# Folding the output weights on array quarters, and another order of loads at the start, in a two-branch linear attention kernel

## The chip, the cores and the metric

The kernel runs on one core of one Trainium2 chip. The metric is the device time of one execution in microseconds. The kernel before takes 189.27 us (median of three executions, 189.26 to 189.87). All six of its executions, 188.97 to 189.87 us, agree within 0.5%. A difference counts as faster or slower when it is 2% or more, which is 3.8 us here.

## The reference

Two branches, A and B, read the same x (2048 tokens of 640 features). Each has its own weights and 32 heads of 20 features, and a gate mixes the results. Cut to what matters:

```python
def branch(x, wqkv, wo):                       # A and B alike
    q, k, v = split(x @ wqkv)                  # 32 heads, Dh = 20
    phi = lambda t: where(t > 0, t + 1, exp(t)) + 1e-6
    kv  = einsum("bhsd,bhse->bhde", phi(k), v) # 20 x 20 for each head
    z   = phi(k).sum over tokens
    o   = (phi(q) @ kv) / (phi(q) . z + 1e-6)
    return o @ wo
out = g * branch_A(x) + (1 - g) * branch_B(x)  # g = sigmoid(x . gate_w)
```

The tokens are divided into 16 tiles of 128. The kernel never makes o. For each branch it forms a 640 x 640 matrix W', the block-diagonal kv times wo, and then makes each output tile as scaled phi(q) times W'.

## The kernel before

A list of operations is handed to a small scheduler that orders them on each engine and assigns PSUM banks. Four parts matter here.

The left factor of W' (KVL) comes from five-step matmuls in units of 120 rows (six heads). VectorE masks it to block-diagonal form:

```python
for us in ((0, 1, 2, 3), (4, 5)):
    ...
    for i, u in enumerate(us):
        lo = GR * u if u < 5 else D - GR          # GR = 120
        for c in range(NC):                       # NC = 5
            e.matmul(PS[0:GR, ps.slot, GR*i : GR*i + GR], WV[X][:, c, lo:lo+GR],
                     gv[:, c, :, lo // 5 : lo // 5 + 24], ...)
    ...   # DVE tensor_tensor: KVL[X][:, us, :] = PSUM * mask
```

W' is one unit of 120 rows at a time. ScalarE copies a unit to WST, and one DMA (a "move") brings it into the layout of WP, in which five rows of WST become one row of 5 x 640:

```python
def wp_unit(X, u):
    e.matmul(a[0:GR, 0:512], KVL[X][:, u, :], WO[X][:, u, 0:512], start=True, stop=True)
    e.matmul(a[0:GR, 512:D], KVL[X][:, u, :], WO[X][:, u, 512:D], start=True, stop=True)
    ...   # ACT: WST[X][:, u, :] = PSUM
    dma("SP", ..., WP[X][lo//5 : hi//5, :, :], WST[X][r:GR, u, :], 1280 * (hi - lo), ...)
```

So a move writes 24 rows of WP and reads 120 rows of WST: 153.6 KB (the profile prints 150.0, in units of 1024 bytes). The last move is a third of that.

The order of branch B's end: the output tiles whose A half is made early ("parts", `o_part`) fill the time until WPB is complete.

```python
kv_unit("B"); o_part(4)
for u in range(NU):                # NU = 6
    wp_unit("B", u)
    if u % 2 == 0: o_part(5 + u // 2)
for t in range(8, NOA): o_part(t)  # NOA = 13; the first matmul on WPB comes right after
```

The start: x tiles 0 and 1 are transposed by TensorE, and the key weights of A arrive in five 128-row pieces.

```python
x_tp(0); warm(6, 1); k_step("A", 0, 0, pss[0])
x_tp(1); k_step("A", 0, 1, pss[0]); k_step("A", 1, 0, pss[1]); k_step("A", 1, 1, pss[1])
gate_col()                          # 5-row transpose of gate_w
... # the other steps of A tiles 0, 1; then B tiles 0, 1; then each tile for A and B
```

## Time and profile before

| | before |
|---|---|
| time | 189.27 us |
| profiled span | 187.4 us |
| TensorE busy | 184.8 us, 99% |
| first matmul on XN and PKA (end of the key stage) | 48.31 us |
| first matmul on WPB | 159.31 us |
| last matmul starts | 185.07 us |

"PE" is TensorE's matmuls and "PEld" its weight loads, which overlap them. The rows by slice cut the span into 40 parts; a digit is the busy share in tenths, and in PEclk the share of the full clock that was granted. A group line gives line, engine, operation, output<-inputs, shape, count, then busy us with mean ns of one, then the idle time just before these instructions and what ended it. A matmul's duration is longer than the distance to the next start (379 ns for 512 columns, with 215 to 216 ns between starts), so TensorE's work is counted by starts. Here are two slice rows and the two groups of output matmuls from the page of the kernel before, for later comparison:

```profile
PE   9999999999999999999999999999999999999995
...
PEclk9999999999999999999999999999999999999999
...
L903 PE MATMUL ps<-WPA,EX 128*128 128x512 bf16 x120 | 17.3, 299 | 0.0
L903 PE MATMUL ps<-WPB,PKA 128*128 128x512 bf16 x120 | 16.5, 299 | 0.0
```

TensorE has no slice below 90% until the end, the clock never falls, and the matmuls on WPB wait for nothing.

### The profile page before, as it was taken

How to read it: one execution, taken by the hardware profiler on the slowest of the kernel's cores; microseconds unless marked ns; L12 is line 12 of the kernel's file. 1: busy time of each engine (PE TensorE's matmuls, PEld its weight loads, DVE VectorE, ACT ScalarE, POOL GpSimd, SP SyncE). 2: the span in 40 equal slices, each digit the busy share in tenths (PEclk: the TensorE clock that was granted, in tenths of full speed). 3: DMA queues.
4: the chain of work that ended last, by engine and by line, in shares of the span. 5: the costliest groups of instructions: out<-in, count | busy, mean ns of one | idle time of the engine just before them, and what ended most of it. 6: DMA issues, size and time to landing. Idle time of an engine off the chain costs nothing.

```text
span 187.4 us, 3207 instructions
## 1 busy us (share of the span) xinstructions
PE 184.8 (99%) x1266; PEld 108.4 (58%) x1266; DVE 136.0 (73%) x263; ACT 94.5 (50%) x168; POOL 0.6 (0%) x7
## 2 busy tenths in 40 slices
PE   9999999999999999999999999999999999999995
PEld 5555555555566656655557556655566655555552
DVE  2489888878833546487798999879996999965600
ACT  3265655565554546644684667877624594100012
POOL 1000000000000000000000000000000000000000
PEclk9999999999999999999999999999999999999999
DMA  7989999999001011011501232540015365132322
GB/s 205 279 162 128 183 381 372 365 227 197 9 0 35 0 38 35 0 35 29 93 9 27 60 48 44 125 113 5 0 37 117 32 152 134 40 138 105 137 79 70
DMA packets 36301, 19.89 MB, mean 106 GB/s; under 512 B 25630, under 2 KB 36286, under 8 KB 36286
## 3 DMA queue, kind: packets, MB, share of 16 engines
q1 hardware_dynamic: 35844, 19.48, 42.9%
q8 instruction: 10, 0.16, 0.4%
q10 hardware_dynamic: 442, 0.20, 0.4%
q14 instruction: 5, 0.04, 0.1%
HBM read 9.39 MB, written 2.62 MB: 64 GB/s over the span
## 4 chain that ended last, share of the span: by engine, by line
PE 99%; DVE 0%; issue 0%; DVEq 0%
PE ps L903 23%; PE ps L743 23%; PE ps L508 19%; PE ps L617 18%; PE ps L618 5%; PE ps L509 5%; PE ps L659 2%; PE ps L442 1%; PE ps L697 1%; PE ps L455 1%; PE ps L698 0%; DVE TSB L947 0%; DVE ONE L372 0%; PE ps L489 0%; DVEq L230 0%
## 5 line engine op out<-in xcount | busy, mean ns | idle before, releaser
L508 PE MATMUL ps<-WKW,XT 128*128 128x512 bf16 x160 | 44.2, 381 | 0.0
L760 ACT ACTIVATE EK<-ps 128x512 bf16<-128x512 f32 x40 | 23.9, 598 | 31.6 <-PE ps L743 29.2
L509 PE MATMUL ps<-WKW,XT 128*128 128x128 bf16 (+1 forms) x160 | 35.2, 220 | 0.0
L541 ACT ACTIVATE EK<-ps 128x640 bf16<-128x640 f32 x32 | 22.3, 703 | 11.6 <-PE ps L509 5.7
L508 PEld LDWEIGHTS ps<-WKW,XT 128*128 128x128 bf16 x160 | 15.7, 98 | 18.9 <-DMA WKW<-in_A_wqkv_dram 0.4
L743 PE MATMUL ps<-XT,WQA 128*128 128x512 bf16 x100 | 24.5, 379 | 0.0
L743 PE MATMUL ps<-XT,WQB 128*128 128x512 bf16 x100 | 23.7, 379 | 0.0
L617 PE MATMUL ps<-XN,PKB 128*128 128x512 bf16 x80 | 23.5, 379 | 0.0
L617 PE MATMUL ps<-XN,PKA 128*128 128x512 bf16 x80 | 23.5, 379 | 0.0
L770 DVE TENSOR_SCALAR EK<-EK 128x512 bf16<-128x512 bf16 x40 | 11.6, 291 | 14.9 <-ACT EK L760 14.6
L618 PE MATMUL ps<-XN,PKA 128*128 128x129 bf16 x80 | 17.6, 220 | 0.0
L618 PE MATMUL ps<-XN,PKB 128*128 128x129 bf16 x80 | 17.6, 220 | 0.0
L903 PE MATMUL ps<-WPA,EX 128*128 128x512 bf16 x120 | 17.3, 299 | 0.0
L903 PE MATMUL ps<-WPB,PKA 128*128 128x512 bf16 x120 | 16.5, 299 | 0.0
L743 PEld LDWEIGHTS ps<-XT,WQB 128*128 128x128 bf16 x100 | 11.0, 118 | 8.5
L509 PEld LDWEIGHTS ps<-WKW,XT 128*128 128x128 bf16 x160 | 15.7, 98 | 0.0
L544 DVE TENSOR_SCALAR EK<-EK 128x640 bf16<-128x640 bf16 x32 | 10.4, 325 | 7.2 <-ACT EK L541 6.9
L743 PEld LDWEIGHTS ps<-XT,WQA 128*128 128x128 bf16 x100 | 10.7, 118 | 8.1
L617 PEld LDWEIGHTS ps<-XN,PKA 128*128 128x128 bf16 x80 | 9.4, 117 | 7.9
L617 PEld LDWEIGHTS ps<-XN,PKB 128*128 128x128 bf16 x80 | 9.4, 117 | 7.8
L949 ACT ACTIVATE TSB<-ps 128x640 bf16<-128x640 f32 (+1 forms) x3 | 2.0, 668 | 23.2 <-PE ps L903 23.2
L552 DVE SCALAR_TENSOR_TENSOR PKB<-ps,EK 128x640 bf16<-128x640 f32 x16 | 13.2, 825 | 0.6
(75 smaller groups left out, 240.6 us busy)
## 6 DMA issues: line engine op xcount, KB each, us to landing
out_dram<-TSB SPq DMA_DIRECT2D x15, 160.0 KB, 1.8
XN<-in_A_x_dram SPq DMA_DIRECT2D x1, 2240.0 KB, 8.8
WKW<-in_A_wqkv_dram SPq DMA_DIRECT2D x5, 160.0 KB, 4.1
WKW<-in_B_wqkv_dram SPq DMA_DIRECT2D x5, 160.0 KB, 4.3
WQA<-in_A_wqkv_dram SPq DMA_DIRECT2D x1, 800.0 KB, 10.5
WQB<-in_B_wqkv_dram SPq DMA_DIRECT2D x1, 800.0 KB, 13.2
WVA<-in_A_wqkv_dram SPq DMA_DIRECT2D x1, 800.0 KB, 12.7
WVB<-in_B_wqkv_dram SPq DMA_DIRECT2D x1, 800.0 KB, 14.2
```

What stands on the lines that cost most here:

```text
L508: e.matmul(a[:, 0:512], l, WK[X][:, c, 0:512], start=(c == 0), stop=(c == NC - 1))
L509: return e.matmul(a[:, 512:w], l, WK[X][:, c, 512:w], start=(c == 0), stop=(c == NC - 1))
L541: op("ACT", lambda e: e.activation(EK[:, ek.slot, :], psw(ps, D), ACT.Exp), act_cost(D), ins=[ps] + first, outs=[ek], name="ke")
L544: lambda e: e.tensor_scalar(EK[:, ek.slot, :], EK[:, ek.slot, :], 1.0, EPS, op0=ALU.min, op1=ALU.add),
L552: lambda e: e.scalar_tensor_tensor(PKt[X][:, t, :], psw(ps, D), 0.0, EK[:, ek.slot, :], op0=ALU.max, op1=ALU.add),
L617: e.matmul(a[:, 0:512], l, XN[:, t, 0:512], start=(t == 0), stop=(t == NT - 1))
L618: return e.matmul(a[:, 512 : D + 1], l, XN[:, t, 512 : D + 1], start=(t == 0), stop=(t == NT - 1))
L659: r = e.matmul(PS[0:GR, ps.slot, GR * i : GR * i + GR], WV[X][:, c, lo : lo + GR], gv[:, c, :, lo // 5 : lo // 5 + 24], start=(c == 0), st ...
L743: r = e.matmul(PS[:, ps.slot, :], WQ[X][:, c, g::5], XT[:, c, 512 * b : 512 * b + 512], start=(c == 0), stop=(c == NC - 1),)
L760: lambda e: e.activation(EQ[:, eq.slot, :], PS[:, ps.slot, :], ACT.Exp),
L770: lambda e: e.tensor_scalar(EQ[:, eq.slot, :], EQ[:, eq.slot, :], 1.0, EPS, op0=ALU.min, op1=ALU.add),
L903: r = e.matmul(a[:, l0 - lo : h0 - lo], PQ[X, b][:, g, 128 * (t % 4) : 128 * (t % 4) + 128], WP[X][:, g, l0:h0], start=(X == first and g = ...
```

## The change

The intent is to take work from TensorE, the bound. A W' unit uses 120 x 120 of the 128 x 128 array for a matrix that is zero outside 20 x 20 blocks. The change cuts W' into 11 tiles of 60 rows (the last 40), and works on four of them at once on the 64 x 64 quarters, in two bursts of 320 output columns per branch. The left factor gets padded rows so that a pair of tiles starts at partitions 0 and 64. The start is reordered, so that x tile 1 is loaded first on ScalarE's queue and transposed right behind tile 0. The gate column becomes a full-array matmul, and A's tile 2 comes before B's keys. In the diff, cuts are marked with `...`:

```diff
-    for u in range(NU):
-        wp_unit("B", u)
-        if u % 2 == 0:
-            o_part(5 + u // 2)
+    wp_burst("B", 0)
+    o_part(5)
+    o_part(6)
+    wp_burst("B", 1)
+    o_part(7)
...
-    NOA = 13
+    NOA = 14
...
+    def wp_burst(X, half):
+        ps = [Buf("wp", "ps", 2) for _ in range(2)]      # two pairs of banks
+        lo = HALF * half                                  # HALF = 320
+        def fn(e):
+            for k in range(3):
+                for a, b in ((0, 192), (192, HALF)) if k == 1 else ((0, HALF),):
+                    for t in range(4 * k, min(4 * k + 4, 11)):
+                        ...                               # c, r: which quarter
+                        x = e.matmul(o[:, HALF*k + a : HALF*k + b],
+                            KVL[X][64*r : 64*r + w, u, d : d + p],
+                            WO[X][64*r : 64*r + w, u, lo + a : lo + b], start=True, stop=True)
+        op("PE", fn, 640.0, ins=bkvl[X] + ...)            # all masks of the branch
+        ...                                               # ACT copies 124 x 960 to WST
+            if half == 0: continue
+            for t in ...:
+                h, m = 64 * (t // 2 % 2), 12 if t < 10 else 8
+                dma("ACT" if X == "B" and t in (1, 5, 9) else "SP", ...,
+                    WP[X][12*t : 12*t + m, :, :], WST[X][h : h + NC*m, 3*r + t//4, :], ...)
...
-                            PS[0:GR, ps.slot, GR * i : GR * i + GR],
-                            WV[X][:, c, lo : lo + GR],
+                            PS[0:n, ps.slot, GR * i : GR * i + NC * w],   # n = 128, last 104
+                            WV[X][:, c, lo : lo + n],
...
-    warm(6, 1)
-    k_step("A", 0, 0, pss[0])
+    warm(1, 1)
     x_tp(1)
-    k_step("A", 0, 1, pss[0])
-    k_step("A", 1, 0, pss[1])
-    k_step("A", 1, 1, pss[1])
+    for c in range(2):
+        for t in range(2):
+            k_step("A", t, c, pss[t])
...
-        op("PE", lambda e: e.transpose(tv(), GW5[:, :], IDN[0:NC, 0:NC]), ...)
+        op("PE", lambda e: e.matmul(tv(), GWZ[:, :], IDN[:, 0:NC], ...), ...)
```

Six moves of 24 rows become eleven of 12 rows (the last 8), all of them after the second burst, on two queues for branch B.

More of the change, by code (lines that the diff above doesn't have):

```diff
@@ L20 @@
 NU = 6
+HR = 60
+HALF = 320
 def _bf16_bits(a):
@@ L30, in _consts @@
     p = np.arange(128)[:, None]
-    bd = (p // 20 == np.arange(24)[None, :] // 4).astype(np.float32)
-    return _bf16_bits(bd)
-CW = 24
+    q, m = p % 64, np.arange(24)[None, :]
+    bd = np.where(p < 64, (q >= 4) & ((q - 4) // 20 == m // 4), (q < 60) & (3 + q // 20 == m // 4))
+    be = q // 20 == m[:, 0:8] // 4
+    return _bf16_bits(np.concatenate([bd, be], axis=1).astype(np.float32))
+CW = 32
 XS_W = 672
@@ L40, with __init__ @@
 class Buf:
-    def __init__(self, name, pool=None, n=1):
-        self.name, self.pool, self.n = name, pool, n
+    def __init__(self, name, pool=None, n=1, at=(0, 2, 4, 6)):
+        self.name, self.pool, self.n, self.at = name, pool, n, at
         self.writers, self.readers = [], []
@@ L107, in can @@
                 w = max(w, d.end + (HOP if d.eng != o.eng or d.dma else 0.0))
+            skip = set()
             for b in o.outs:
                 if b.pool and b.slot is None:
-                    got = self.pick(b, w)
+                    got = self.pick(b, w, skip)
                     if got is None:
@@ L113, in can @@
                     w = max(w, got[0])
+                    skip |= set(range(got[1], got[1] + b.n))
             return w
@@ L163, in run, with pick @@
         return max(o.end for o in self.ops)
-    def pick(self, b, t):
+    def pick(self, b, t, skip=()):
         pool = self.free[b.pool]
@@ L169, in pick @@
         for x in pool:
-            have[x[1]] = x[0]
+            if x[1] not in skip:
+                have[x[1]] = x[0]
         if b.n == 1:
-            if not pool:
+            if not have:
                 return None
@@ L176, in pick @@
             return best[0], best[3]
-        c = [(max(have[s], have[s + 1]), s) for s in have if s % 2 == 0 and s + 1 in have]
+        c = [(max(have[i] for i in range(s, s + b.n)), s) for s in b.at if all(i in have for i in range(s, s + b.n))]
         return min(c) if c else None
@@ L275, in body @@
     WQ = {X: sb("WQ" + X, [128, NC, D], bf) for X in XS}
-    WV = {X: sb("WV" + X, [128, NC, D], bf) for X in XS}
-    WO = {X: sb("WO" + X, [GR, NU, D], bf) for X in XS}
+    WV = {X: sb("WV" + X, [128, NC, D + 8], bf) for X in XS}
+    WO = {X: sb("WO" + X, [128, NU, D], bf) for X in XS}
     PK = {X: sb("PK" + X, [128, NT * D], bf) for X in XS}
@@ L296, in body @@
     GS = {X: sb("GS" + X, [128, NC, D], bf) for X in XS}
-    KVL = {X: sb("KVL" + X, [GR, NU, GR], bf) for X in XS}
-    WST = {X: WKW[0:GR, i * NU * D : (i + 1) * NU * D].rearrange("p (u f) -> p u f", u=NU) for i, X in enumerate(XS)}
+    KVL = {X: sb("KVL" + X, [128, NU, GR], bf) for X in XS}
+    WST = {X: WKW[:, i * NU * D : (i + 1) * NU * D].rearrange("p (u f) -> p u f", u=NU) for i, X in enumerate(XS)}
     WP = {X: sb("WP" + X, [128, NC, D], bf) for X in XS}
@@ L303, in body @@
     FXT = {"A": WV["A"][:, :, :].rearrange("p c f -> p (c f)")[:, 0:2048].rearrange("p (b s) -> p b s", b=NB), "B": XNf[:, 0:2048].rearrange("p (b s) -> p b s", b=NB)}
-    NOA = 13
+    NOA = 14
     OA = [XNf[:, 2048 + 1280 * i : 3328 + 1280 * i].bitcast(f32) for i in range(6)]
-    OA += [PK["B"][:, 1280 * i : 1280 * i + 1280].bitcast(f32) for i in range(7)]
+    OA += [PK["B"][:, 1280 * i : 1280 * i + 1280].bitcast(f32) for i in range(8)]
     NEK, NEQ, NOS = 4, 4, 4
@@ L318, in body @@
     CST = sb("CST", [128, CW], bf)
-    GW5 = sb("GW5", [NC, 128], bf)
+    GWZ = sb("GWZ", [128, 128], bf)
     GE = sb("GE", [128, NT], f32)
@@ L328, in body @@
     IDN = sb("IDN", [128, 128], bf)
-    BDM = CST[0:GR, 0:24]
+    BDM = CST[:, 0:24]
+    BDE = CST[64:104, 24:32]
     sch = Sched({"ps": 8, "ek": NEK, "eq": NEQ, "os": NOS})
@@ L369, in body @@
     bwv = {X: Buf("wv" + X) for X in XS}
-    bwo = {X: Buf("wo" + X) for X in XS}
+    bwo = {}
     op("DVE", lambda e: e.memset(ONE[:, :], 1.0), 120.0, outs=[bone], name="one")
@@ L385, in body @@
     )
+    bpad = {X: Buf("pad") for X in XS}
+    for X in XS:
+        op("POOL", lambda e, X=X: e.memset(WV[X][:, :, 0:4], 0.0), 100.0, outs=[bpad[X]], prio=10**6, name="wvpad")
+        op("POOL", lambda e, X=X: e.memset(WO[X][0:4, 0:5, :], 0.0), 1500.0, outs=[bpad[X]], prio=10**6, name="wopad")
+    zgw = op("POOL", lambda e: e.memset(GWZ[:, :], 0.0), 200.0, name="zgw")
     bxo = Buf("xo")
@@ L410, in body @@
     bgw = Buf("gw5")
+    ld_x("ACT", 1)
+    dma("ACT", "gw", GWZ[0:NC, :], gate_w.rearrange("(c p) -> c p", p=128), 1280, outs=[bgw], after=[zgw])
     dma("ACT", "cst", CST[:, :], cap[:, :], 128 * CW * 2, outs=[bcst])
-    ld_x("ACT", 1)
-    dma("ACT", "gw", GW5[:, :], gate_w.rearrange("(c p) -> c p", p=128), 1280, outs=[bgw])
     for c in range(NC):
@@ L417, in body @@
         ld_wk("SP", "A", c)
+    xt_dma(2, 3)
     for c in range(NC):
         ld_wk("SP", "B", c)
-    for t0, t1 in ((2, 3), (3, 4), (4, 5), (5, 6), (6, 8), (8, 12), (12, 16)):
+    for t0, t1 in ((3, 4), (4, 5), (5, 6), (6, 8), (8, 12), (12, 16)):
         xt_dma(t0, t1)
@@ L425, in body @@
     for X in XS:
-        dma("SP", "wv" + X, WV[X][:, :, :], w3(X, 2), 819200, outs=[bwv[X]])
+        dma("SP", "wv" + X, WV[X][:, :, 4 : D + 4], w3(X, 2), 819200, outs=[bwv[X]])
     for X in XS:
-        bo5 = Buf("wo5" + X)
-        dma("SP", "wo" + X, WO[X][:, 0:5, :], wo[X][0:600, :].rearrange("(u p) n -> p u n", p=GR), 768000, outs=[bwo[X]])
-        dma("SP", "wo5" + X, WO[X][:, 5, :], wo[X][520:640, :], 153600, outs=[bo5])
-        bwo[X, 5] = bo5
+        for r in range(2):
+            bwo[X, r] = Buf("wo")
+            dma(
+                "SP",
+                "wo%s%d" % (X, r),
+                WO[X][4 + HR * r : 64 + HR * r, 0:5, :],
+                wo[X][0:600, :].rearrange("(u r p) n -> r p u n", r=2, p=HR)[r],
+                384000,
+                outs=[bwo[X, r]],
+            )
+        bwo[X, 2] = Buf("wo")
+        dma("SP", "wo2" + X, WO[X][64:104, 5, :], wo[X][600:640, :], 51200, outs=[bwo[X, 2]])
     loading.clear()
@@ L467, in x_tp, with copy @@
             half = Buf("xth")
-            op(
-                "DVE",
-                lambda e, lo=lo, hi=hi, bt=bt: e.tensor_copy(
-                    XT[:, lo:hi, 128 * t : 128 * t + 128],
-                    PS[:, bt.slot, 0 : 128 * (hi - lo)].rearrange("p (c s) -> p c s", c=hi - lo),
-                ),
-                dve1(128 * (hi - lo)),
+            def copy(e, lo=lo, hi=hi, bt=bt):
+                o = XT[:, lo:hi, 128 * t : 128 * t + 128]
+                i = PS[:, bt.slot, 0 : 128 * (hi - lo)].rearrange("p (c s) -> p c s", c=hi - lo)
+                return e.activation(o, i, ACT.Copy) if t else e.tensor_copy(o, i)
+            op(
+                "ACT" if t else "DVE",
+                copy,
+                act_cost(128 * (hi - lo)) if t else dve1(128 * (hi - lo)),
                 ins=[bt],
@@ L486, in tv @@
         def tv():
-            return PS[:, bt.slot, :].bitcast(bf)[:, 0:NC]
-        op("PE", lambda e: e.transpose(tv(), GW5[:, :], IDN[0:NC, 0:NC]), 60.0, ins=[bgw, bid], outs=[bt], name="gwt")
+            return PS[:, bt.slot, 0:NC]
+        op("PE", lambda e: e.matmul(tv(), GWZ[:, :], IDN[:, 0:NC], start=True, stop=True), 60.0, ins=[bgw, bid], outs=[bt], name="gwt")
         op(
@@ L580, in body @@
         k_post("A", t, pss[t])
-    pss = [Buf("k", "ps", 2) for _ in range(2)]
-    for c in range(NC):
-        for t in range(2):
-            k_step("B", t, c, pss[t])
-    for t in range(2):
-        k_post("B", t, pss[t])
-    for t in range(2, NT):
+    k_unit("A", 2)
+    for t in range(3):
+        k_unit("B", t)
+    for t in range(3, NT):
         for X in XS:
@@ L651, in kv_unit, with out @@
         gv = GS[X][:, :, :].rearrange("p c (g m) -> p c g m", g=NC)
-        for us in ((0, 1, 2, 3), (4, 5)):
-            ps = Buf("kv", "ps")
-            def fn(e, us=us, ps=ps):
-                for i, u in enumerate(us):
-                    lo = GR * u if u < 5 else D - GR
-                    for c in range(NC):
-                        r = e.matmul(
-                            PS[0:GR, ps.slot, GR * i : GR * i + GR],
-                            WV[X][:, c, lo : lo + GR],
-                            gv[:, c, :, lo // 5 : lo // 5 + 24],
-                            start=(c == 0),
-                            stop=(c == NC - 1),
-                        )
-                return r
-            o = op("PE", fn, 5 * len(us) * mm_cost(GR), ins=[bwv[X]] + [bgs[X, g] for g in range(NC)], outs=[ps], name="kv" + X)
-            if X == "A":
-                kv_op[X].append(o)
+        def out(src, u0, n, w, mask, r0, r1):
             b = Buf("kvl")
             bkvl[X].append(b)
-            n = len(us)
             op(
                 "DVE",
-                lambda e, us=us, ps=ps, n=n: e.tensor_tensor(
-                    out=KVL[X][:, us[0] : us[0] + n, :].rearrange("p u (m g) -> p u g m", g=NC),
-                    in0=PS[0:GR, ps.slot, 0 : GR * n].rearrange("p (u g m) -> p u g m", u=n, g=NC),
-                    in1=BDM.unsqueeze(1).unsqueeze(1).to_broadcast([GR, n, NC, 24]),
+                lambda e: e.tensor_tensor(
+                    out=KVL[X][r0:r1, u0 : u0 + n, 0 : w * NC].rearrange("p u (m g) -> p u g m", g=NC),
+                    in0=src().rearrange("p (u g m) -> p u g m", u=n, g=NC),
+                    in1=mask.unsqueeze(1).unsqueeze(1).to_broadcast([r1 - r0, n, NC, w]),
                     op=ALU.mult,
                 ),
-                dve1(GR * n),
+                dve1(w * NC * n),
                 ins=[ps, bcst],
@@ L687, in kv_unit, with fn @@
             )
-    bwp = {}
+        for us in ((0, 1, 2, 3), (4, 5)):
+            ps = Buf("kv", "ps")
+            def fn(e, us=us, ps=ps):
+                for i, u in enumerate(us):
+                    for c in range(NC):
+                        lo, n, w = (GR * u, 128, 24) if u < 5 else (540, 104, 8)
+                        r = e.matmul(
+                            PS[0:n, ps.slot, GR * i : GR * i + NC * w],
+                            WV[X][:, c, lo : lo + n],
+                            gv[:, c, :, 24 * u : 24 * u + w],
+                            start=(c == 0),
+                            stop=(c == NC - 1),
+                        )
+                return r
+            o = op("PE", fn, 5 * len(us) * 55.0, ins=[bwv[X], bpad[X]] + [bgs[X, g] for g in range(NC)], outs=[ps], name="kv" + X)
+            if X == "A":
+                kv_op[X].append(o)
+            n = min(us[-1], 4) - us[0] + 1
+            out(lambda ps=ps, n=n: PS[:, ps.slot, 0 : GR * n], us[0], n, 24, BDM, 0, 128)
+            if 5 in us:
+                out(lambda ps=ps: PS[64:104, ps.slot, GR : GR + 40], 5, 1, 8, BDE, 64, 104)
@@ L690, in body @@
+    bwst = {(X, r): Buf("wst") for X in XS for r in range(2)}
     bwpm = {X: [] for X in XS}
-    def wp_unit(X, u):
-        ps = Buf("wp", "ps", 2)
+    def wp_burst(X, half):
+        ps = [Buf("wp", "ps", 2) for _ in range(2)]
+        lo = HALF * half
         def fn(e):
-            a = psw(ps, D)
-            e.matmul(a[0:GR, 0:512], KVL[X][:, u, :], WO[X][:, u, 0:512], start=True, stop=True)
-            return e.matmul(a[0:GR, 512:D], KVL[X][:, u, :], WO[X][:, u, 512:D], start=True, stop=True)
-        op(
-            "PE",
-            fn,
-            mm_cost(512) + mm_cost(128),
-            ins=[bkvl[X][u // 4], bwo[X] if u < 5 else bwo[X, 5]],
-            outs=[ps],
-            name="wp%s%d" % (X, u),
-        )
-        b = Buf("wst")
-        op(
-            "ACT",
-            lambda e: e.activation(WST[X][:, u, :], psw(ps, D)[0:GR, :], ACT.Copy),
-            act_cost(D),
-            ins=[ps],
-            outs=[b],
-            prio=-1,
-            name="wpc",
-        )
-        bwp[X, u] = b
-        d = Buf("wpm")
-        bwpm[X].append(d)
-        r = 80 if u == 5 else 0
-        lo, hi = GR * u, min(D, GR * u + GR)
-        dma(
-            "SP",
-            "wpm%s%d" % (X, u),
-            WP[X][lo // 5 : hi // 5, :, :],
-            WST[X][r:GR, u, :],
-            1280 * (hi - lo),
-            ins=[b],
-            outs=[d],
-            issue=850.0,
-            prio=-1,
-        )
@@ new lines, in fn @@
+            for k in range(3):
+                for a, b in ((0, 192), (192, HALF)) if k == 1 else ((0, HALF),):
+                    for t in range(4 * k, min(4 * k + 4, 11)):
+                        c, r, u = t // 2 % 2, t % 2 if t < 10 else 1, t // 2
+                        w, p = (64 - 4 * r, HR) if t < 10 else (40, 40)
+                        d = HR * r if t < 10 else 0
+                        o = PS[64 * c : 64 * c + p, ps[r].slot : ps[r].slot + 2, :].rearrange("p a b -> p (a b)")
+                        x = e.matmul(
+                            o[:, HALF * k + a : HALF * k + b],
+                            KVL[X][64 * r : 64 * r + w, u, d : d + p],
+                            WO[X][64 * r : 64 * r + w, u, lo + a : lo + b],
+                            start=True,
+                            stop=True,
+                        )
@@ new lines, in fn @@
+            return x
+        op("PE", fn, 640.0, ins=bkvl[X] + [bwo[X, i] for i in range(3)] + [bpad[X]], outs=ps, name="wp%s%d" % (X, half))
+        for r in range(2):
+            op(
+                "ACT",
+                lambda e, r=r: e.activation(
+                    WST[X][0:124, 3 * r : 3 * r + 3, lo : lo + HALF],
+                    psw(ps[r], 3 * HALF)[0:124, :].rearrange("p (k n) -> p k n", k=3),
+                    ACT.Copy,
+                ),
+                act_cost(3 * HALF),
+                ins=[ps[r]],
+                outs=[bwst[X, r]],
+                prio=-1 if X == "A" else None,
+                name="wpc",
+            )
+            if half == 0:
+                continue
+            for t in [t for t in range(11) if (t % 2 if t < 10 else 1) == r]:
+                d = Buf("wpm")
+                bwpm[X].append(d)
+                h, m = 64 * (t // 2 % 2), 12 if t < 10 else 8
+                dma(
+                    "ACT" if X == "B" and t in (1, 5, 9) else "SP",
+                    "wpm%s%d" % (X, t),
+                    WP[X][12 * t : 12 * t + m, :, :],
+                    WST[X][h : h + NC * m, 3 * r + t // 4, :],
+                    6400 * m,
+                    ins=[bwst[X, r]],
+                    outs=[d],
+                    issue=650.0,
+                    prio=None if X == "B" and t in (1, 5, 9) else -1,
+                )
@@ L1003, in f @@
             elif g == 2:
+                if k == 2:
+                    wp_burst("A", 1)
                 q_next(1)
-                wp_unit("A", 2 * k)
-                wp_unit("A", 2 * k + 1)
+                if k == 0:
+                    wp_burst("A", 0)
             elif g == 3:
```

## The prediction

> **What bounds the kernel now.** I read the page first: engine shares, the granted clock by slice, and the chain of work that ended last. The clock row is 9 throughout, so nothing here is about throttling.
>
> ```profile
> PE 184.8 (99%) x1266; PEld 108.4 (58%) x1266; DVE 136.0 (73%) x263; ACT 94.5 (50%) x168; POOL 0.6 (0%) x7
> ...
> PE 99%; DVE 0%; issue 0%; DVEq 0%
> ```
>
> The chain is TensorE from end to end, so only three things can move the time: TensorE work removed, new waits of TensorE, or a different start or tail. A busy PE need not be at its peak, so I then took the differences of matmul starts in the trace. From the third load of A's key weights (first matmul at 6.39 us) to the last matmul (185.07 us) every start follows its predecessor by 0.215 us per 512 columns or 0.055 us per 128. There is no gap left; the profiled span of 187.4 us ends 2.3 us after that with the last copies and stores.
>
> The groups by line and form give the parts that the change touches:
>
> ```profile
> L697 PE MATMUL ps<-WOB,KVLB 120*120 120x512 bf16 x6 | 2.1, 380 | 0.0
> ...
> L659 PE MATMUL ps<-GSB,WVB 128*120 128x120 bf16 x30 | 1.8, 218 | 0.0
> ...
> L676 DVE TENSOR_TENSOR KVLB<-ps,CST 120x480 bf16<-120x480 f32 x1 | 1.5, 1501 | 1.4 <-PE ps L659 1.4
> ...
> L698 PE MATMUL ps<-WOB,KVLB 120*120 120x128 bf16 x6 | 1.3, 217 | 0.0
> ...
> L676 DVE TENSOR_TENSOR KVLB<-ps,CST 120x240 bf16<-120x240 f32 x1 | 0.9, 910 | 0.0
> ```
>
> L697 and L698 make W' (6 units of 512+128 columns per branch), L659 makes its left factor, L676 masks that factor into KVL. [...]I count by start spacing: a W' unit takes 0.272 us of TensorE, so 6 x 0.272 = 1.63 us per branch; the 30 matmuls of L659 run from 100.38 to 102.03, 1.65 us per branch.
>
> The timeline of TensorE and its weight loads shows the start:
>
> ```profile
> 4.16 0.55 PE L455 MATMUL ps<-IDN,XN 128*128 128x128 bf16 x5
> ...
> 4.74 0.10 PEld L508 LDWEIGHTS ps<-WKW,XT 128*128 128x128 bf16 x1 [0.21 <-DMA WKW<-in_A_wqkv_dram]
> ...
> 5.52 0.22 PE L509 MATMUL ps<-WKW,XT 128*128 128x128 bf16 x1
> ...
> 5.67 0.17 PE L489 MATMUL ps<-IDN,GW 5*128 5x5 bf16 x1
> ...
> 5.78 0.39 PE L508 MATMUL ps<-WKW,XT 128*128 128x512 bf16 x1
> ...
> 6.39 0.10 PEld L508 LDWEIGHTS ps<-WKW,XT 128*128 128x128 bf16 x1 [0.23 <-DMA WKW<-in_A_wqkv_dram]
> ```
>
> TensorE waits for the second and the fourth 128-row piece of A's key weights (they land at 4.70 and 6.35 us by their semaphores). The 5-row transpose of the gate column costs far more than 5 columns: 0.15 us instead of 0.055 before it, 0.11 us after it, so about 0.1 us for each change of array shape (it is also a transpose, so the two are not separated).
>
> And the timelines around the second branch's W', VectorE then TensorE:
>
> ```profile
> 145.10 2.17 DVE L676 TENSOR_TENSOR KVLB<-ps,CST 120x480 bf16<-120x480 f32 x2 [1.38 <-PE ps L659]
> 147.02 0.91 DVE L850 RECIPROCAL DNT<-DNT 128x128 f32<-128x128 f32 x1
> ```
>
> ```profile
> 143.80 1.81 PE L659 MATMUL ps<-GSB,WVB 128*120 128x120 bf16 x30
> 145.45 1.52 PE L903 MATMUL ps<-WPA,EX 128*128 128x512 bf16 x10
> 146.80 0.38 PE L697 MATMUL ps<-WOB,KVLB 120*120 120x512 bf16 x1
> ```
>
> The first mask ends at 146.60 and the first W' unit, which needs only that one, starts at 146.80: 0.2 us of slack. The second mask ends at 147.27, under cover.
>
> [...]The 120-column loads here already take 133 to 135 ns against 98 to 118 for 128 columns, and are hidden all the same.
>
> **The change part by part.**
>
> W' bursts. 7680 columns of full-array matmul, 3.27 us over both branches, go. Each of four bursts has 11 tiles x 320 columns on four quarters: three rounds of 320 columns (the middle one as 192+128[...]). If quarters overlap, three rounds x 320 columns x 0.42 ns = 0.40 us; two mode changes x 0.1 = 0.2; staggered starts of 15 load/matmul pairs, say 0.04. Estimate 0.64 us a burst, 2.56 us in all: saving 0.71 us.
>
> Left factor. Units become 128 wide in the weights but still stream 120 columns (25 matmuls), the last one 40 columns (5 matmuls). 25 x 0.0535 + 5 x 0.035 = 1.51 us (0.035 is my estimate[...]) against 1.65: saving 0.14 x 2 = 0.28 us.
>
> New wait. A burst needs all of KVL of its branch, not its unit's part. In the order of the changed kernel TensorE does the factor, one output part, then the burst; VectorE does three masks of 480, 120 and 40 elements. Before, one 480 mask held VectorE 1.26 us until the next began and one of 240 held it 0.66, so 2.6 to 2.75 ns an element: 0.33 for 120, and the last, 40 elements, ends about 0.35 after it starts (0.1 plus the 0.25 by which the 910 ns exceeds 0.66). In the old time frame: 145.10 + 1.26 + 0.33 + 0.35 = 147.04, plus about 0.06 of hand-over, 147.10. TensorE would arrive at 146.80 - 0.14 = 146.66. Wait 0.45 us, on the chain. Branch A has some 13 us between factor and burst, so none there.
>
> B's W' placement. The rows reach WPB only after the second half has been copied: ScalarE copies of 960 elements (0.70 us for 640 gives about 0.97), then eight moves on SP and three on ScalarE's queue. SP took 0.77 us to issue a 24-row move and 0.69 for an 8-row one, so about 0.71 for 12 rows; a move landed about 3 us after its issue began. Second burst ends near 151.1, first half of the copies 152.3, last issue 152.35 + 7 x 0.71 = 157.3, landing 160.3. TensorE, with seven output parts of 1.36 us behind that burst, asks for WPB at 151.1 + 9.5 = 160.6. It fits by 0.3 us, less than the error of the sum: I charge 0.1.
>
> Start. Tile 1's transposes move ahead of the first key matmuls, its copies go to ScalarE (idle then), and tile 1's first key step fills the wait for the second weight piece. But TensorE then stands again at the fourth piece, which has the same bytes ahead of it as before, and whatever was gained earlier (also the 0.2 us of the gate column) is lost there. Earlier issue of x tile 1 (0.13 instead of 0.51 us) may bring all loads forward by 0.1. Against that A's tile 2 is now wanted at about 7.49 us; its transposing DMA goes right behind the fifth weight piece, which landed at 6.82, and the first such DMA before landed 0.66 after the piece ahead of it: 7.48, a coin toss; I charge 0.1. B's pieces, one DMA later, are wanted from 8.85 instead of 7.49, which covers their delay. Net zero.
>
> Sum: -0.71 - 0.28 + 0.45 + 0.1 + 0.0 = -0.44 us on 189.27: 188.8. One output tile more through the two-part path (14 instead of 13) is the same matmul columns.
>
> **The rivals.** (1) The quarters do not overlap. For: nothing in this trace shows overlap.[...] Then a burst is 3520 columns x 0.42 = 1.48 plus drains, 1.7 us, four of them 6.8 instead of 3.27; with the other terms about 192.7. (2) The start really gains. For: two waits and a slow gate step stand there; if pieces three to five land as fast as the ones after them (0.4 us apart instead of 0.8), up to 0.7 us comes out: about 188.1. Against: the DMA engines are busy from 1 us on, and no bytes are removed. (3) The waits win: if WPB lands 1 us late or tile 2 lands 0.5 us late, the saving is eaten: 189.3 to 189.9. (4) PSUM: a burst takes four of eight banks at once. For: q units also hold banks beside it. Against: ScalarE is only half busy, and the bank assignment in the built order shows bursts on pairs freed well before. I give it nothing.
>
> **Range and chances.** All likely outcomes lie between 188.0 and 189.9, the best start with no waits to both waits long. Two per cent is 3.8 us; only 6.5 us of TensorE work is touched and the floor of the rest is unmoved, so faster by 2% is nearly excluded; slower by 2% needs rival 1 together with a wait.
>
> **What would show it.** Right: burst from first to last matmul start plus its neighbours' gap near 0.64 us; a gap of about 0.45 us before B's first burst with the mask as releaser; none before A's; factor 1.5 us; key steps dense from about 6.4 us with at most one short wait for XT. Wrong: bursts over 1 us (rival 1), the dense stretch starting well before 6.2 us (rival 2), or a gap before the first matmul on WPB over 0.3 us (rival 3).

## The result, and the profile after

The changed kernel takes 192.00 us (median of six executions, 191.38 to 192.95). The kernel before, run beside it on the same chip, takes 189.26. A ratio here is the mean time of one kernel's runs over that of the other's of the same rounds, so it is not quite the ratio of the medians. It is 1.0149, with a 95% interval of 1.0108 to 1.0190. That is within 2%, but clearly a loss, and outside the predicted range of 188.0 to 189.9.

The six executions fall into two groups. Three took 191.38 to 191.44 us with a mean granted clock of 1.0, and three took 192.57 to 192.95 with 0.991. The profiled one (192.93) is of the second group. From its page, the engine shares, the slices, the chain by engine, and the two groups shown above:

```profile
PE 185.6 (97%) x1297; PEld 107.5 (56%) x1297; DVE 136.2 (71%) x263; ACT 94.9 (50%) x167; POOL 6.2 (3%) x12
...
PE   8999999999999999999999999999999995899995
...
PEclk9999999999999999999999999999999999699999
...
PE 91%; DMA 3%; ACT 2%; DVE 1%; ACTq 1%; issue 1%; SPq 0%; DVEq 0%
...
L942 PE MATMUL ps<-WPB,PKA 128*128 128x512 bf16 x120 | 17.9, 315 | 2.8 <-DMA WPB<-WKW 2.8
...
L942 PE MATMUL ps<-WPA,EX 128*128 128x512 bf16 x120 | 17.0, 299 | 0.0
```

There is a hole in TensorE's row in the slices 34 and 35 (counted from 1), and the clock is down in slice 35. The chain, all TensorE before, has DMA in it. The group on WPB has 2.8 us of idle time in front, ended by the DMA that fills WPB, and its mean has gone from 299 to 315 ns while the same matmul on WPA stays at 299. The same matmuls take longer on WPB, and the clock granted between 163.40 and 167.00 us was 0.59.

The timeline of TensorE where WPB is first used, of the kernel before and of the changed one (columns: start, duration from first to last of a stretch, what, count, idle before):

```profile
157.96 1.52 PE L903 MATMUL ps<-WPA,PKA 128*128 128x512 bf16 x10
159.31 8.86 PE L903 MATMUL ps<-WPB,PKA 128*128 128x512 bf16 x64
```

```profile
157.65 2.88 PE L942 MATMUL ps<-WPA,PKA 128*128 128x512 bf16 x20
163.35 4.83 PE L942 MATMUL ps<-WPB,PKA 128*128 128x512 bf16 x23 [2.82 <-DMA WPB<-WKW]
```

The changed kernel has one output part more ahead of this point (1.36 us, moved and not added). Before would therefore have been here at 159.31 + 1.36 = 160.67, and after is ready at 160.37 (its last part's final matmul starts at 160.31). So **0.30 us was gained up to this point, and then 2.99 us is lost at once**. The chain of waits of the changed kernel names the piece:

```profile
157.76 5.43 DMA WPB<-WKW
163.19 0.17 issue
163.35 2.72 PE ps L942 x9
```

The eleventh and smallest move of W' is issued at 157.76, about when I expected the last issue (157.3), but takes 5.43 us to land instead of some 3. The table by stretch (columns: stretch, its length, busy us and count of PE, PEld, DVE, ACT and POOL, then PEclk, DMA share and GB/s) shows what the wait draws after it:

```profile
160.00:163.40 3.40, 0.58 (x5) 0.23 (x4) 0.00 (x0) 0.70 (x1) 0.00 (x0) 0.93 1.32 106
163.40:167.00 3.60, 3.60 (x17) 1.70 (x18) 2.35 (x3) 0.00 (x0) 0.00 (x0) 0.59 0.03 3
```

The DMA share is the time that packets took, over that of 16 engines. A value of 1.32 means that packets' times overlap on an engine. I take that for a first sign of a queue.

While TensorE waited, its clock was cut. In the trace the granted clock is 0.5 from 162.96 to 166.37, 3.413 us. In that time 512-column matmuls start 0.427 us apart instead of 0.216, and 128-column ones 0.107 instead of 0.056. The sum of these excesses is 1.47 us. That is close to the distance of the two groups of executions: 192.93 - 191.39 = 1.54.

Next, the moves themselves. The time from a move's issue to the last semaphore step of its landing, by the trace:

| moves of B's W' | first | in the middle | last | mean time of a 1280-byte packet |
|---|---|---|---|---|
| before, 24 rows, SP alone | 3.40 us | 3.44 us | 3.09 us (8 rows) | 71 ns |
| after, 12 rows, SP and ScalarE | 3.12 us | 5.00 us (the sixth) | 5.43 us (8 rows), 6.16 us the one before | 141 ns on SP's queue, 148 on ScalarE's |
| after, branch A, 12 rows, SP alone | 3.28 us | 3.30 us | 2.69 us (8 rows) | 73 ns |

The moves queue up: from the third to the ninth that lands (157.06 to 161.75 us) there is one landing per 4.69 / 6 = 0.78 us, which is 76.8 KB / 0.78 us = 98 GB/s. Before, the first three moves land 0.85 us apart with 153.6 KB each, 181 GB/s. That is no limit of the moves: SP issues them 0.82 us apart, so they land about as fast as they are issued.

Lastly the bursts and the mask. TensorE's timeline of the changed kernel, around A's first burst, then B's:

```profile
115.06 0.60 PE L732 MATMUL ps<-WOA,KVLA 64*60 64x320 bf16 x15
...
143.43 1.69 PE L699 MATMUL ps<-GSB,WVB 128*128 128x120 bf16 x30
...
146.95 0.60 PE L732 MATMUL ps<-WOB,KVLB 64*60 64x320 bf16 x15 [0.47 <-DVE KVLB L679]
```

and two of the three masks of B, from its groups by form:

```profile
L679 DVE TENSOR_TENSOR KVLB<-ps,CST 128x120 bf16<-128x120 f32 x1 | 0.6, 587 | 0.0
...
L679 DVE TENSOR_TENSOR KVLB<-ps,CST 40x40 bf16<-40x40 f32 x1 | 0.3, 274 | 0.0
```

Fifteen matmuls of up to 320 columns in 0.60 us, where 3520 columns one after another would take 1.48 us at 0.42 ns each (0.215 us for 512): the quarters do work side by side. B's burst waits for the mask, A's does not.

### The profile page after: what moved, and what is told of

It reads as the page before. It is cut to its first block, busy times and chain, and to the rows that moved or that the text cites.

```text
span 191.5 us, 3296 instructions
## 1 busy us (share of the span) xinstructions
PE 185.6 (97%) x1297; PEld 107.5 (56%) x1297; DVE 136.2 (71%) x263; ACT 94.9 (50%) x167; POOL 6.2 (3%) x12
## 4 chain that ended last, share of the span: by engine, by line
PE 91%; DMA 3%; ACT 2%; DVE 1%; ACTq 1%; issue 1%; SPq 0%; DVEq 0%
PE ps L782 23%; PE ps L533 18%; PE ps L638 18%; PE ps L942 18%; PE ps L534 5%; PE ps L639 5%; DMA WPB<-WKW 3%; PE ps L699 1%; ACTq L351 1%; PE ps L464 1%; DVE KVLB L679 1%; ACT PKB L966 1%; ACT WKW L745 1%; PE ps L732 1%; PE ps L477 1%
## 5 line engine op out<-in xcount | busy, mean ns | idle before, releaser
L533 PE MATMUL ps<-WKW,XT 128*128 128x512 bf16 x160 | 44.8, 385 | 0.0
L942 PE MATMUL ps<-WPB,PKA 128*128 128x512 bf16 x120 | 17.9, 315 | 2.8 <-DMA WPB<-WKW 2.8
L942 PEld LDWEIGHTS ps<-WPB,PKA 128*128 128x128 bf16 x120 | 9.7, 102 | 11.1 <-issue 4.8
L988 ACT ACTIVATE TSB<-ps 128x640 bf16<-128x640 f32 (+1 forms) x2 | 1.3, 650 | 27.0 <-PE ps L942 27.0
```

The source lines that it names most:

```text
L533: e.matmul(a[:, 0:512], l, WK[X][:, c, 0:512], start=(c == 0), stop=(c == NC - 1))
L942: r = e.matmul(a[:, l0 - lo : h0 - lo], PQ[X, b][:, g, 128 * (t % 4) : 128 * (t % 4) + 128], WP[X][:, g, l0:h0], start=(X == first and g = ...
```

## The experiments

The theory after reading the traces: the loss is the wait for WPB, because moves of 12 rows pass no faster than one per 0.78 us, plus the clock cut that such a wait can bring. The rivals: the start loses, the number of moves or the second queue is at fault, or something else holds TensorE there. Where nothing else is said, a median is of several executions on one chip beside 11 of the kernel before (medians 189.18 to 189.28).

### The start alone

Edit: the kernel before with the new loads, gate column and key order, and no change to W'.

> The kernel before with the start of the change alone (x tile 1 first on ScalarE's queue, its transposes behind tile 0's and copied by ScalarE, the full-array gate matmul, A's tile 2 before B). Theory: the whole loss of the change lies at the arrival of WPB, and the start gains what the trace of the changed kernel shows, its tile-2 key step at 7.285 us where the kernel before was equally far at 7.491: 0.2 us, so about 189.05. Rival: the later release of the clock (5.94 us in the changed kernel's trace against 4.37) comes from the new start and costs: then this kernel is not faster than before, 189.3 or more.

Measured: 188.92 us (188.55 to 191.31, six executions; one of the six took 191.31 at full clock, which nothing recorded explains), ratio 1.0008 (0.9966 to 1.0051). In the profiled execution the key stage ends at 48.06 us instead of 48.31, and the last matmul starts at 184.81 instead of 185.07, so the 0.25 us carries through. But that stage's end varies between executions: in four traces with the old start it is 47.92, 48.31, 48.68 and 49.06, and in eight with the new start it is 48.06 to 48.41. The start loses nothing. Whether it gains some 0.2 us on average these runs do not settle.

### The W' part alone

Edit: the changed kernel with the loads, gate column and key order of before.

> The changed kernel with the old start put back: W' on quarters alone. Theory: it waits for WPB as the changed kernel does, about 3 us, and in runs in which the clock falls after that wait another 1.5: 191.6 or 193.1. Rival: the loss comes from the two parts together: then about 189.

Measured: 192.90 us (192.03 to 193.45, four), ratio 1.0192 (1.0164 to 1.0220). The gap before the first matmul on WPB is 3.04 us from start to start, as in the changed kernel (2.99 us of it is wait), and the clock fell in three of the four executions. The loss is in the W' part.

### Bursts for A, full-array units for B

Edit: branch B keeps `wp_unit` with its 24-row moves and its two masks; all else is as changed. I call this the mixed version.

```diff
-    kv_unit("B"); o_part(4); wp_burst("B", 0); o_part(5); o_part(6); wp_burst("B", 1); o_part(7)
+    kv_unit_full("B"); o_part(4)
+    for u in range(NU):
+        wp_unit("B", u)
+        if u % 2 == 0: o_part(5 + u // 2)
```

> The changed kernel with branch B's W' as before (six full-array units, moves of 24 rows, mask of 120 partitions); branch A keeps its two bursts, the start is the new one. Theory: no wait for WPB and none for B's mask, so start 0.2, A's factor 0.15 and A's bursts 1.63 - 2 x 0.66 = 0.3 come out: 188.6. Rival: quarters are themselves the loss (they disturb what follows, in either branch): then over 189.3.

Measured: 188.91 us (188.72 to 189.27, five), ratio 0.9987 (0.9968 to 1.0005). Neither WPB nor the mask is waited for, and the clock stays at 1.0. TensorE now waits 0.36 us at 9.53 us for B's fifth piece of key weights, which is why 188.6 was missed. Taking away B's bursts removes the whole loss, and A's bursts and moves, which nobody waits for, do no harm.

### One output part more ahead of WPB

```diff
-    NOA = 14
+    NOA = 15   # with a buffer for it in WQ["A"]
```

> The changed kernel with 15 output tiles by the two-part path instead of 14 (one more buffer, in A's spent query weights): TensorE asks for WPB 1.36 us later, the moves are unchanged. Theory: the last move's landing sets the time, so the wait shrinks from 3.0 to about 1.65 us, the clock no longer falls, and the time is 191.4 - 1.36 = about 190.05, the same in all executions. Rival: TensorE stands for another reason (an output buffer, a scaled query tile): then the wait stays near 3 us and the time at 191.4 to 192.9.

Measured: 190.50 us (190.18 to 191.00, four), ratio 1.0072 (1.0049 to 1.0094). The clock stayed at 1.0 in all four. The chain of waits of this run:

```profile
157.43 5.46 DMA WPB<-WKW
162.90 0.25 issue
163.14 2.88 PE ps L943 x20
```

TensorE does 1.36 us more work first, and still starts on WPB at 163.14. The landing sets the time, not TensorE. The gap, from start to start, is 1.80 us (1.65 expected). The step from the full-clock executions of the changed kernel (191.4) is 0.9 us where 1.2 is the difference of the gaps; the start and the tail vary by as much.

### Before, with B's moves halved by rows, and halved by columns

Both take the kernel before and cut each 24-row move of B in two, the second half issued by ScalarE. Count, bytes and issuers are the same in both; only the shape differs.

```diff
 rows:     WP[X][lo//5 + 12*i : lo//5 + 12*i + 12, :, :]      <- WST[X][60*i : 60*i + 60, u, :]
 columns:  WP[X][lo//5 : hi//5, :, 320*i : 320*i + 320]       <- WST[X][r:GR, u, 320*i : 320*i + 320]
```

> The kernel before, with each of branch B's first five W' moves (24 rows of WPB x 640 columns) cut into two moves of 12 rows, the second of each pair issued by ScalarE: 11 moves as in the changed kernel, but started as early as before. Theory: a move into 12 rows drains slowly (about 0.75 us each when several are in flight, packets of 1280 B at 140 to 170 ns instead of 70)[...], so landings stretch from 3 to 4 us or more after issue, the last lands near 160, and TensorE, which asks at 159.3, waits 0.5 to 1 us. Rival, queueing is not special to 12 rows: no wait, landings 3 us after issue.

> The same count of moves, bytes, issuers and order, but each pair cut by columns: 24 rows x 320 columns. Theory of few rows: these drain about twice as fast as the 12-row moves, land about 3 us after issue and the last by 159; no wait, 189.2. Rival, the count of moves (a fixed cost of each, its completion) or two issuing queues is to blame: landings as late as with 12 rows, and the same wait.

Measured, rows: 194.11 (clock 0.991) and 191.84 (clock 1.0), ratio 1.0195 (1.0141 to 1.0250). Columns: 190.02 and 189.77, ratio 1.0033 (1.0005 to 1.0061). The chain of waits of the first, and TensorE's timeline of the second:

```profile
157.43 4.73 DMA WPB<-WKW
162.16 0.67 issue
162.83 3.34 PE ps L914 x14
```

```profile
160.42 4.78 PE L914 MATMUL ps<-WPB,PKA 128*128 128x128 bf16 x34 [0.21 <-issue]
```

In halves by rows, a 1280-byte packet takes 118 to 120 ns, the time from issue to landing grows from 3.2 us (3.8 for the first move) to 5.3 us, and the last move lands at 162.16. That is later than the 160 expected, and the gap, 2.46 us from start to start, is longer than the 0.5 to 1 us expected. In halves by columns the 640-byte packets take 36 to 37 ns, a move lands 2.4 to 3.1 us after its issue throughout, the last at 159.75, and some 0.4 us of gap is left. The kernel before is thus made slow by the cut by rows, with two executions of each to show it. The number of moves and the second queue by themselves are nearly harmless. The profiled execution of the first had a late start as well (key stage done at 49.06), so its time overstates the effect, though its landing does not.

### All eleven moves on SP

```diff
-                    "ACT" if X == "B" and t in (1, 5, 9) else "SP",
+                    "SP",
```

> The changed kernel with all eleven of B's moves issued by SP alone. Theory: the moves drain at about 0.75 us each whoever issues, SP issues one in 0.77, so the last still lands near 152.1 + 10 x 0.77 + 3 = 162.8 and the wait is 2.5 to 3 us as before; time 191 to 193. Rival, two queues disturb each other: packets fall back to about 70 ns, but issue then sets the same end. What tells them apart is the packet time and the latency of each move: 3 us under the rival, growing to 4 or more under the theory.

Measured: 190.98 us (190.92, 190.97, 190.98 at full clock, and 192.60 at 0.991), ratio 1.0110 (1.0077 to 1.0144). The end of the chain of waits:

```profile
160.16 0.04 issue
160.20 2.67 DMA WPB<-WKW
162.87 0.14 issue
```

The time to landing stays at 3.1 us and falls to 2.7, packets take 72 ns, and the last move lands at 162.87, against 163.19 with two queues. My expectation took growing times to landing for the mark of the theory and steady ones for the mark of the rival (two queues disturb each other), and by that mark the rival won. But the mark was badly chosen: SP issues one move per 0.81 us, just slower than the 0.78 us at which they land when queued, so under the theory too no queue need form after the issue. The test does not separate the two. It shows that the three moves on ScalarE's queue bought nothing, and that 12-row moves from one queue land as fast as before. The run by columns shows that a second issuer does no harm to moves of 24 rows (2.4 to 3.1 us to landing). What is slow is the two together: moves of 12 rows, issued by two queues and so faster than one per 0.81 us.

### Three bursts by tiles, moves after each

Edit: each burst does four tiles over all 640 columns, so that its moves start at once, and the first two need only the first mask.

> The changed kernel with W' in three bursts per branch that are cut by tiles (4, 4 and 3 tiles, all 640 columns) instead of two cut by columns: the first tiles' moves start three microseconds earlier, and the first burst needs only the first mask. Three bursts of about 0.27 + 0.25 us instead of two of 0.66. Theory: the cause is only that moves start late and drain slowly, so no wait for WPB and nearly none for the mask: about 188.5 against 189.2 of before. Rival: eleven 12-row moves are too many even so: a wait of 1 us or more remains, 189.5 or more.

Measured: 190.11 us (189.92 to 190.79, six), ratio 1.0049 (1.0028 to 1.0070). The wait for the mask is gone, and the wait for WPB is down to a gap of 0.57 us. But the third burst and the part behind it wait for ScalarE's copies, with gaps of 0.72 and 0.58 us from start to start, and the copies are held up by ScalarE's own DMA issues of 0.8 to 0.9 us each. The 188.5 was missed: one wait had become two others.

### The mixed version with another key order

```diff
-    for t in range(3):
-        k_unit("B", t)
+    for c in range(NC):             # tiles 0 and 1 take each key piece in turn
+        for t in range(2):
+            k_step("B", t, c, pss[t])
+    ...
+    k_unit("B", 2)
```

> The hybrid (A in bursts on quarters, B's W' as before, new start) with one more edit: after A's tile 2, B's tiles 0 and 1 take each piece of B's key weights in turn, as the kernel before did, so that the last piece is wanted about 1 us later. In the hybrid's trace TensorE stood 0.36 us for that piece. Theory: that wait goes, nothing else changes: 0.2 to 0.35 us below the hybrid where the clock comes early, so 188.6, and the interval against the kernel before lies wholly below 1. Rival: the wait moves to another load or the gain drowns in the start's variation: 188.9, interval over 1.

Measured: 188.95 us (188.60 to 189.36, six), ratio 0.9984 (0.9967 to 1.0000). In the profiled run the wait for B's fifth piece is gone, but TensorE stands for A's second piece until 5.04 us (0.59 us) and for a PKA copy until 9.16 (0.28). The wait has moved to another load and to a copy.

### The second burst earlier, and the two bursts joined

Both have fifteen parts, as in the fourth run, and move B's second burst ahead: by one part, or right behind the first burst.

```diff
     wp_burst("B", 0)
-    o_part(5)
-    o_part(6)
-    wp_burst("B", 1)
+    wp_burst("B", 1)        # joined; the other version leaves o_part(5) between
+    o_part(5)
+    o_part(6)
```

> The version with fifteen output tiles in two parts (wait for WPB 1.80 us, 190.5 us), and B's second burst moved ahead by one output part (1.36 us). Theory (the queue of twelve-row moves sets when WPB is complete): all moves shift by 1.36 us, the last lands near 161.8, the wait shrinks from 1.80 to about 0.45 us, time 190.5 - 1.36 = 189.15; the moves' latency still grows from 3 to some 6 us; the clock does not fall. Rival (the moves are held by something later in the program, or PSUM takes the gain): the wait stays above 1 us or a gap of over 0.5 us opens beside the second burst, 189.7 or more.

> As the run before, with B's two bursts one right behind the other, all output parts after them. Theory: moves another 1.36 us earlier, the last lands near 160.4, no wait for WPB is left, and one pair of mode changes falls away (0.2 us); 188.6 to 188.8, the 0.3 to 0.5 us that the prediction hoped for and thus the fastest of all. Rival (PSUM: two bursts fill all eight banks, so the next output part stands until ScalarE has copied one pair, 0.97 us a copy): a gap of 0.5 to 1.0 us opens behind the second burst and the time is 189.1 to 189.6.

Measured: 189.50 us (189.18 to 190.13, six), ratio 1.0014 (0.9988 to 1.0040), and 189.45 us (189.18 to 189.58, six), ratio 1.0005 (0.9979 to 1.0030). With one part between, the last move lands at 162.41 (161.8 expected) and the gap before WPB is 0.77 us from start to start (0.45 expected), so the 189.15 was missed. Joined, all moves are in by 161.26 and no wait for WPB is left, as the theory says, but TensorE's timeline shows two new ones:

```profile
148.47 5.61 PE L943 MATMUL ps<-WPA,EX 128*128 128x512 bf16 x40 [0.65 <-ACT WKW L746]
154.37 0.93 PE L943 MATMUL ps<-WPA,EX 128*128 128x512 bf16 x5 [0.30 <-ACT XN L967]
```

Two joined bursts hold all eight PSUM banks, so the next part waits for ScalarE's copy (the gap is 0.81 us beyond the normal spacing). Later a part waits for a copy that stands behind ScalarE's DMA issues (0.46 us). The rival of that expectation was right. No version tried is clearly faster than the kernel before; the two mixed ones come closest, at 0.13 and 0.16% below it, with intervals that reach 1.0 or beyond.

## Why the prediction was wrong

The working was a sum, and its terms can be checked one by one in the profiled execution after:

| term | predicted | measured |
|---|---|---|
| four bursts for twelve units | -0.71 us | -0.65 us |
| left factor, both branches | -0.28 us | -0.23 us |
| wait for the mask, B | +0.45 us | +0.54 us |
| start | 0.0 us | +0.07 us |
| wait for WPB | +0.1 us | +2.99 us |
| clock cut after that wait | not foreseen | +1.47 us, in half of the executions |
| sum | -0.44 us | +4.19 us |

The last matmul starts at 189.21 instead of 185.07 us, 4.14 us later, so the table closes to within 0.05.

**The bursts.** Right. A burst of A costs 0.66 us and one of B 0.64, against 0.64 predicted: 3.26 - 2 x 0.66 - 2 x 0.64 = 0.66, or 0.65 unrounded. Rival 1 falls: the quarters do overlap (fifteen matmuls in 0.60 us, where one after another would take 1.48). Until the result this was an assumption; no trace before shows it. Each change between the full array and the quarters costs about 0.095 us: around A's first burst the starts are 0.309 us apart, less 0.215 for 512 columns, before it, and 0.230, less 0.135 for 320, after it. The 0.04 for staggered starts was a guess; beside the two changes and the 0.40 of columns, 0.05 to 0.07 is left.

**The left factor.** Mechanism right, size a little off. The 40-column matmuls, after the first, start 0.048 to 0.049 us apart, where I had estimated 0.035, and those of 120 columns 0.052 to 0.053, where I had put 0.0535. The trace of the kernel before shows neither figure of mine; starts of 120 columns are 0.055 apart in it. It takes 1.53 us a branch instead of 1.65.

**The mask.** Right. The gap before B's first burst is 0.69 us in matmul starts; less the normal 0.055 and the mode change of 0.095, the mask is 0.54. The two small masks took 587 and 274 ns. The hand-over to TensorE, for which I had guessed 0.06, took 0.14.

**The start.** Right within what can be told. The key stage ends at 48.37 us instead of 48.31, less than the variation between executions. The expected short wait for tile 2 did not come, but in this execution the full clock came later, at 5.94 us instead of 4.37.

**B's W' placement: the step that failed.** It said "a move landed about 3 us after its issue began" and "It fits by 0.3 us, less than the error of the sum: I charge 0.1." The issue came where I had it within half a microsecond, and so did TensorE's demand (160.37 against 160.6). What I carried over wrongly was the 3 us. It had been read from moves on one queue, whose time to landing hardly grew (3.4 to 3.7 us for 24 rows, 3.1 for the last of 8), and it was put on moves of half the rows issued from two queues, as if the time to landing were a constant and not the end of a queue. It measured 5.43 us for the last move, 6.16 for the one before. Of the 2.89 us between the predicted landing at 160.3 and the real one at 163.19, 0.46 is the later issue and 2.43 the longer time to landing. The pair by rows and by columns shows that the shape of a move matters once two queues issue (up to 5.3 us to landing by rows, 3.1 by columns). With SP alone the time to landing stays near 3 us, but the issues take so long that the last landing, at 162.87, is hardly earlier.

The runs show 98 to 106 GB/s for queued moves of 12 rows (one landing per 0.78 us here, per 0.72 us with the second burst one part earlier) and, for 24 rows, at least 181, the rate at which they were issued. Why queued moves of fewer rows go slower is not shown. A move of 12 written rows also reads 60 rather than 120, and the halves by columns differ from those by rows in their packets too (640 bytes, not 1280); no run separates these. One number does not fit a plain limit of the rows: with SP alone, the 60 packets of a 12-row move take 0.52 us from the first start to the last end, which is 147 GB/s. With two queues packets grow longer over SP's first five moves (72, 73, 118, 164 and 214 ns on average), and those on SP's queue stay long (201 ns between 158.5 and 159.5 us) after the last one of ScalarE's moves has ended at 158.51. Open too is what holds back the last landing: the last data packet of the moves ends 1.64 us before it, and with SP alone 0.90. DMA transposes that SP issues from 158.49 on share its queue, and no run takes them away.

**The clock.** Nothing in the prediction foresaw it. Each cut was to a granted clock of 0.5 and lasted 3.413 us, and the stretches of full clock before the four cuts lasted 157.013 us (three times) and 160.426 us, which is 46 and 47 times 3.413. In the 3.413 us before each cut, TensorE had been idle for 2.1 to 2.7 us. In the version with fifteen parts, a wait of 1.58 us brought no cut. What decides between a cut and none in executions of one kernel is not shown. By the length of the wait: versions whose profiled gap is 2.5 to 3.0 us from start to start had the cut in some of their executions (three of six of the changed kernel, three of four of the W' part alone, one of two of the cut by rows, one of four with all moves on SP), and versions with 1.8 us or less in none. The waits of the executions without a profile are not known.

**Rival 3** named the right place, "if WPB lands 1 us late", but sized it at a third and ended the range at 189.9. The result is within 2% all the same, as the prediction had argued, because so little of the kernel's work is touched.

**Two slips** in the working change nothing in its argument: the matmul at 6.39 us belongs to the fourth piece of A's key weights, not to the third, and rival 1's own terms add up to 193.1 us, not 192.7.

## What to carry to other kernels

When a change makes DMA transfers smaller or narrower and issues them faster, do not carry over their time to landing: it can be the end of a queue (here it went from some 3 us to 5.43 and 6.16), so find out how fast such transfers land one after another and compare that with how fast they are issued. A work saving of half a microsecond on the bounding engine is only worth having if everything that engine waits for keeps its slack, and cutting work into bursts uses slack up, since each burst needs all of its inputs, all of its banks, and gives all of its outputs late. Look at the clock after a long wait as well: here a wait of 2.99 us on TensorE came with 3.413 us at half clock, which cost another 1.47 us, and three of the six executions had such a cut.
